# Attention and two gated MLPs on one core: scores in three 64-row passes, sums unfolded, another clock in the planner

## The chip, the cores and the metric

The kernel runs on one core of one Trainium2 chip. The metric is the time of one execution on the device, in microseconds (us). The engines are TensorE (PE in the profile, PEld for its weight loads), VectorE (DVE), ScalarE (ACT), GpSimd (POOL) and SyncE (SP), whose queue issues nearly all DMAs.

## What is computed

The inputs are q, k and v for 4 batches, 12 heads, 448 positions and a head size of 64, in float32. The reference, cut to what matters:

```python
q_n, k_n = rmsnorm(q, g_q), rmsnorm(k, g_k)          # x / sqrt(mean(x*x)+1e-6) * g
attn = softmax(q_n @ k_n.T / 8)
x = (attn @ v), heads side by side                    # 4 x 448 x 768
h = relu(x @ w_in); c = conv over 3 positions of h    # d_ff 1024
x = (h * sigmoid(c)) @ w_out
g = sigmoid(causal conv over 5 positions of x)
out = (g * (x @ w_val)) @ w_out2
```

## The kernel before

Products are taken in float16 with each operand split in a high and a low part: high times high, high times low and low times high are summed in PSUM.

Heads are handled in pairs. A *unit* is 128 query rows of a pair of heads (kind "full", 72 units) or the last 64 rows of two pairs (kind "rem", 12 units); there are 21 units in each of the 4 batches. `prep` makes q and k ready for two pairs: it loads them, sums their squares (`sum_q`, `sum_k`), takes the inverse root in a few steps on VectorE (`rroot`), multiplies k with the gains and its root (`gain_k`, `norm_k`), and splits q and k in halves (`split_q`, `norm_k`, `low_k`). DMA transposes (`turn_q`, `turn_k`) bring them to the layout with the head dimension on partitions: `qa` and `ka`. In `norm_k` the high part of k is copied a second time, so that each head's column block of `ka` has it on rows 0 to 63 and again on rows 64 to 127; `qa` has for each head q's high and low part under each other, so one matmul over 128 rows gives high k times (high q + low q). `qk` issues this for both heads, and then the low part of k times high q over 64 rows, for one head on rows 0 to 63 and for the other on rows 64 to 127. It writes to one of two PSUM buffers, `ps_s`, with one bank for each head.

`sum_q` and `sum_k` square on ScalarE or GpSimd and call `total`. With FOLD_Q = FOLD_K = 2 `total` first adds halves of the 64 squares on GpSimd, twice, and reduces the 16 that are left on VectorE. The first group of pairs, marked solo, isn't folded.

After the scores, `smax` takes the negative maximum on VectorE, `sexp` the exponential on ScalarE. For a unit with `u.out` set, the exponentials go to an SBUF buffer, `phi` copies them to float16 and `plo` subtracts on VectorE or GpSimd; otherwise the exponentials overwrite the scores in PSUM, and `plo` is a VectorE instruction that reads PSUM. OUT = (0, 4, 4, 4) sets `u.out` for all units of batches 1 to 3. The units of batch 0 are `wide`: their probabilities stay in float32 and TensorE transposes them. In the other batches DMA transposes turn p into `pt`, and `av` multiplies with v. The MLP of batch b runs beside the attention of batch b+1; the MLP of batch 3 runs alone.

The order of the instructions is made by the program itself, on the host, in the class `Plan`. Every instruction is recorded with the time at which the program wants it. `order` is a list scheduler: it keeps a clock for each engine with an estimated duration for each instruction (`cost`), and lets each engine take the ready instruction with the smallest value of `first`, a mix of the wanted time and of the length of the chain behind it (URGENT). Instructions given for two engines go to the one that would end sooner, with a lean. A change of matmul shape on TensorE is made less likely by SWITCH. `clocked` models the granted clock. The result is one fixed queue for each engine, in which every instruction waits for those ahead of it. All these instructions have line 351 in the profile, since `emit` issues them there.

Of the kernel before, what the change touches and what calls it, by code (L numbers as in the profile page):

```python
# [9 lines left out]
F32 = mybir.dt.float32  # L10
F16 = mybir.dt.float16
# [14 lines left out]
class Plan:  # L26
# [10 lines left out]
    HOP = {"tensor": 0.2, "vector": 0.13, "scalar": 0.16, "gpsimd": 0.09}  # L37
    WINDOW = 23.2
    AHEAD = 55.6
    URGENT = 0.598  # L40
    TICK = 10.24 / 3
    ENTRY = 3060.0

    SWITCH = 3.692

    KEEP = 0.1
# [123 lines left out]
    def cost(self, engine, method, a, k, aps, out):  # L170
# [63 lines left out]
    def order(self):  # L234
        ops, nops = self.ops, len(self.ops)
        users = [[] for _ in ops]
        left = [len(o[1]) for o in ops]
        for i, o in enumerate(ops):
            for d in o[1]:
                users[d].append(i)  # L240
        ready = [o[2] for o in ops]
        tail = [0.0] * nops
# [12 lines left out]
        first = [o[4] * (1.0 - self.URGENT) - tail[i] * self.URGENT for i, o in enumerate(ops)]  # L255
        waiting = {e: [] for e in Plan.ENGINES}
        free = dict.fromkeys(Plan.ENGINES, 1.05)
# [22 lines left out]
        while len(result) < nops:  # L280
# [36 lines left out]
            if method.startswith("dma"):  # L317
                if e != "gpsimd":
                    t = max(since + 0.03 if e == "scalar" else t, ready[i], hwdge)
                    hwdge = t + lag + 0.03  # L320
                    busy = max(free[e] - t, lag + 0.05)
                    dma = max(dma, hwdge + 0.62)
                    if method == "dma_start_transpose":
                        busy = max(1.22, dma + 0.69 - t if data > 1.0 else 0.0)
                    dma += data
                else:
                    dma = max(dma, t + 3.4) + data
                end = dma + (0.7 if k["out"].space == bass.MemoryType.DRAM else 1.5)
            else:
                end = t + busy + lag  # L330
            if e == "scalar":
                since = t
            free[e] = t + busy
            if port[i][e]:
                held[e] = t + busy - (0.06 if e == "vector" else 0.09)
            result.append((t, len(result), i, e))
            for u in users[i]:
# [3 lines left out]
                if left[u] == 0:  # L341
                    enter(u)
        self.length = max(free.values())
        self.times = {i: t for t, _, i, _ in result}
        self.engine = {i: e for _, _, i, e in result}
        return [(i, e) for _, _, i, e in result]

# [7 lines left out]
def kernel(  # L355
# [43 lines left out]
    wo, wv, w2 = (sb.tile([P, 2 * n, DM], F16, tag=t, name=t) for t, n in (("wo", KF), ("wv", KD), ("w2", KD)))  # L399
    ka = tiles(NKA, [P, 3, S], F16, "ka")  # L400
    qa = tiles(2, [P, NQ, P], F16, "qa")
    vvf = tiles(NV, [P, 2 * NB * (D + 1)], F16, "vv")
# [9 lines left out]
    qin = tiles(1, [P, NQ, D], F32, "qin")  # L412
    tk = tiles(1, [KR, 3, KC, 2 * D], F16, "tk")
    tq_ = tiles(1, [P, NQ, 2 * D], F16, "tq")
    p32 = tiles(2, [P, 2, S], F32, "p32_")
# [55 lines left out]
    START = 8.8  # L471
    HOLD = 12.4
    EARLY_W = 19
# [17 lines left out]
    C_LO = 3.1  # L491
    V_HI = 0.971
    A_HI = 0.836
    A_LO = 1.248
    A_OUT = 0.192
    E_PTR = 0.83
    E_AV = 2.135
    X_LAG = 1.732
    MPE = 96.0
    M_0 = 2.65  # L500
    M_1 = 0.311
    M_2 = 0.038
    M_3 = -1.7
    D_IN = 3.4
    L_TAP = 0.0
    L_DUP = 4.061
# [8 lines left out]
    D_OUT = 4.34  # L515
    D_VAL = 3.58
    D_Y = 2.44
    KLEAD = 3.645
    QLEAD = 3.741
    VLEAD = 5.37  # L520
    STAT = 0.341
    KD_ = 1.21
    QD_ = 1.09
    W_IN = -69.458
    W_IN_STEP = 1.774
    W_OUT = -16.897
    W_OUT_STEP = 2.33
    W_VAL = 30.678
    W_VAL_STEP = 2.16
    W_2 = 85.7  # L530
    W_2_STEP = 3.998
# [5 lines left out]
    BIG_2 = 0  # L537
    OUT = (0, 4, 4, 4)
    WIDE_0 = 1
# [7 lines left out]
    L_WLO = 0.899  # L547
    L_ROOT = 0.3
    L_QHI = 0.729
    L_QLO = 0.968  # L550
    L_GAIN = 1.72
    L_NORM = 4.34
    L_KHI = 1.361
    L_KLO = 0.76
    L_PLO = 0.5
    L_VM = 0.001
    L_VHI = 1.224
    L_VLO = 1.058
    L_PHI = 1.118
    L_PT = 4.0  # L560
    L_XHI = -0.2
    L_GHI = 1.0

# [58 lines left out]
    for i in range(EARLY):  # L622
        free.remove(i)
    tk.append(slot(0, 3)[:KR, 0 : 12 * 2 * D].rearrange("p (a c d) -> p a c d", a=3, c=KC))
    early_sq = slot(3, 2).bitcast(F32)
# [155 lines left out]
    def prep(b, r, t0, tq, dq, tk_, dk, ahead):  # L781
# [16 lines left out]
        n = 4 * FULL  # L798
        oh = oq.rearrange("p (n h) (a d) -> p n (h a) d", h=2, a=2)[:, :, 0:4:3]
        gain_b = gb[0][:KR].unsqueeze(1).to_broadcast([KR, 2 * KC, D])  # L800
# [25 lines left out]
        def sum_q():  # L826
            s2 = early_sq if b == 0 else oq.rearrange("p n d -> p (n d)").bitcast(F32)
            s2 = s2.rearrange("p (n d) -> p n d", d=D)
            square(s2, xq)
            total(FOLD_Q, ss[:, 0:NQ], s2)  # L830

        def split_q():
            x = xq.rearrange("p (n h) d -> p n h d", h=2)
            copy(lean(L_QHI, S_LQ), oh, x)
            sub(lean(L_QLO, S_LQ), oq.rearrange("p (n x) d -> p n (x d)", x=2)[:, :, D : 3 * D].rearrange("p n (h d) -> p n h d", h=2), x, oh)

        def turn_q():
            nc.sync.dma_start_transpose(out=qa[g % 2], in_=oq.rearrange("p n d -> p (n d)"))

        def of_k(i):  # L840
            j = 2 * r + i
            x = kin[i]
            o = tk[i if b == 0 else 0]
            return j, x, x.rearrange("p h c d -> p (h c) d"), o, o[:, 0:2]

# [5 lines left out]
        def sum_k(i):  # L851
            j, x, x3, o, hi = of_k(i)
# [11 lines left out]
        def norm_k(i):  # L864
            j, x, x3, o, hi = of_k(i)
            assert holds["kin", i] == (b, j)
            holds["tk", i if b == 0 else 0] = b, j
            vg(lean(L_NORM, S_LK), "tensor_tensor", x3, x3, rr[:KR, cols(i)].unsqueeze(2).to_broadcast([KR, 2 * KC, D]), ALU.mult)
            copy(lean(L_KHI, S_LK), hi[:, :, :, 0:D], x)
            copy(lean(L_DUP, S_LK), hi[:, :, :, D : 2 * D], hi[:, :, :, 0:D])  # L870

        def low_k(i):
            j, x, x3, o, hi = of_k(i)
            assert holds["kin", i] == holds["tk", i if b == 0 else 0] == (b, j)
            sub(lean(L_KLO, S_LK), o[:, 2].rearrange("p c (h d) -> p h c d", h=2), x, hi[:, :, :, 0:D])

        def turn_k(i):
            j, x, x3, o, hi = of_k(i)
# [628 lines left out]
```

## Time and profile before

| | |
|---|---|
| three timed runs | 697.35 us median, 695.71 to 697.99 |
| the profiled execution | 692.04 us, of which 689.8 us is the span of the core |
| granted TensorE clock, mean | 0.955 of full speed |
| TensorE | 589.4 us busy (85% of the span), 4562 matmuls |
| VectorE | 508.4 us (74%), 1072 instructions |
| ScalarE | 432.9 us (63%), 751 |
| GpSimd | 300.7 us (44%), 328 |

A busy time counts the instructions that an engine executes, and for VectorE this includes time in which an instruction has begun and waits inside. The records of successive matmuls overlap, so the price of one is read from the start of one to the start of the next and not from its duration.

### The profile page before, as it was taken

What the parts mean: (1) busy time and instruction counts of PE and PEld (TensorE: products, weight loads), DVE (VectorE), ACT (ScalarE), POOL (GpSimd) and SP (SyncE); (2) the same over time, 40 slices, a digit from 0 to 9 for tenths busy, and PEclk for the clock granted to TensorE, in tenths of its full rate; (3) what the DMA queues carried; (4) which work ended last, traced back from release to release, by engine and by line L of the source; (5) the groups of instructions that cost most, each with busy time, mean ns of one, the idle gap of its engine ahead of it and who ended that gap; (6) DMA issues with size and microseconds to landing.
All of it is one profiled execution on the core that took longest, in us unless ns stands there. A gap on an engine that the chain in (4) does not pass through costs nothing. (4 is left out here: it accounts for less than half of the span.)

```text
span 689.8 us, 12402 instructions
## 1 busy us (share of the span) xinstructions
PE 589.4 (85%) x4562; PEld 333.8 (48%) x4562; DVE 508.4 (74%) x1072; ACT 432.9 (63%) x751; POOL 300.7 (44%) x328
## 2 busy tenths in 40 slices
PE   0579888957787898786989899999999899999997
PEld 0447766434343344343545454654554456545554
DVE  5888977998998877889728586459889763586720
ACT  3588988886886964786837575577856543342211
POOL 3376366666476675564756644441653110000000
PEclk9997999989898999979999999999999999999999
DMA  8968576968977985985978758865836736100001
GB/s 203 219 158 202 126 183 141 219 127 158 219 158 160 234 151 120 193 183 120 168 168 176 123 106 139 164 126 112 146 67 113 115 54 153 35 1 0 1 21 60
DMA packets 269324, 91.76 MB, mean 133 GB/s; under 512 B 255387, under 2 KB 265169, under 8 KB 269265
## 3 DMA queue, kind: packets, MB, share of 16 engines
q1 hardware_dynamic: 268353, 90.76, 63.6%
q8 instruction: 35, 0.57, 0.3%
q10 hardware_dynamic: 912, 0.23, 0.1%
q14 instruction: 24, 0.20, 0.1%
HBM read 38.66 MB, written 5.51 MB: 64 GB/s over the span
## 5 line engine op out<-in xcount | busy, mean ns | idle before, releaser
L351 PE MATMUL psm<-act,wi 128*128 128x448 f16 x576 | 124.2, 363 | 8.9 <-DVE act L351 8.8
L351 ACT ACTIVATE p<-pss,mx,root 128x448 f32<-128x448 f32 x154 | 103.5, 721 | 38.7 <-POOL mx L351 18.7
L351 PE MATMUL psm<-act,wo 128*128 128x448 f16 x576 | 121.7, 358 | 1.6 <-DVE act L351 1.6
L351 PE MATMUL pss<-ka,qa 128*128 128x448 f16 (+3 forms) x384 | 84.4, 376 | 32.2 <-DMA ka<-tk 20.0
L351 DVE TENSOR_REDUCE pss<-pss 128x2 f32<-128x896 f32 x84 | 90.9, 1091 | 24.0 <-PE pss L351 21.5
L351 POOL TENSOR_TENSOR p<-p,p 128x896 f16<-128x896 f32 x41 | 77.7, 1895 | 50.1 <-ACT p L351 38.5
L351 PE MATMUL psm<-act,wv 128*128 128x448 f16 x432 | 92.9, 362 | 5.9 <-DVE act L351 5.9
L351 PE MATMUL psm<-w,act 128*128 128x384 f16 (+1 forms) x576 | 93.2, 327 | 0.9 <-DVE act L351 0.9
L351 ACT ACTIVATE act<-psm 128x448 f16<-128x448 f32 (+4 forms) x97 | 51.4, 536 | 61.2 <-DVE psm L351 42.3
L351 PEld LDWEIGHTS <-wi 128*128 128x128 f16 x576 | 55.9, 100 | 61.9 <-issue 18.2
L351 PEld LDWEIGHTS <-pt 128*128 128x128 f16 (+1 forms) x1512 | 59.5, 103 | 50.4 <-DMA pt<-p 32.0
L351 PEld LDWEIGHTS <-wo 128*128 128x128 f16 x576 | 55.1, 99 | 54.6 <-issue 9.3
L351 PE MATMUL psx<-vv,pt 128*128 128x65 f16 (+1 forms) x1116 | 71.5, 207 | 0.4 <-ACT pt L351 0.4
L351 PEld LDWEIGHTS <-act 128*128 128x128 f16 (+1 forms) x576 | 48.7, 101 | 33.2 <-issue 4.3
L351 DVE SCALAR_TENSOR_TENSOR act<-psm,cw,act 128x444 f32<-128x444 f32 (+3 forms) x96 | 63.7, 676 | 1.0
L351 PEld LDWEIGHTS <-wv 128*128 128x128 f16 x432 | 41.9, 100 | 45.1 <-issue 12.0
L351 PEld LDWEIGHTS <-qa 128*128 128x128 f16 (+3 forms) x384 | 25.3, 100 | 76.1 <-issue 47.6
L351 ACT ACTIVATE p<-p 128x896 f16<-128x896 f32 x62 | 58.9, 950 | 1.8 <-DMA pt<-p 1.3
L351 DVE SCALAR_TENSOR_TENSOR w<-w 128x768 uint32<-128x768 uint32 (+1 forms) x56 | 47.9, 866 | 0.6 <-POOL w L351 0.4
L351 DVE SCALAR_TENSOR_TENSOR scr<-psm,cw,scr 128x447 f32<-128x447 f32 x64 | 43.0, 677 | 4.4 <-ACT scr L351 3.7
L351 PE MATMUL psx<-vm,pt 128*128 128x130 f16 (+1 forms) x186 | 25.1, 241 | 22.2 <-DMA pt<-p 15.7
L351 DVE SCALAR_TENSOR_TENSOR act<-psm,act 128x448 f16<-128x448 f32 x48 | 29.7, 618 | 12.6 <-ACT act L351 12.5
(122 smaller groups left out, 906.0 us busy)
## 6 DMA issues: line engine op xcount, KB each, us to landing
w<-in_moe_w_in_dram SPq DMA_DIRECT2D x8, 768.0 KB, 6.4
w<-in_moe_w_out_dram SPq DMA_DIRECT2D x8, 768.0 KB, 5.9
kin<-in_k_dram SPq DMA_DIRECT2D x23, 224.0 KB, 3.6
qin<-in_q_dram SPq DMA_DIRECT2D x36, 128.0 KB, 3.2
act<-in_moe_w_out_dram SPq DMA_DIRECT2D x12, 384.0 KB, 3.4
w<-in_moe_w_val_dram SPq DMA_DIRECT2D x12, 384.0 KB, 3.9
out_dram<-osb SPq DMA_DIRECT2D x24, 192.0 KB, 2.5
vst<-in_v_dram SPq DMA_DIRECT2D x18, 224.0 KB, 4.3
```

The costliest lines, as they stand in the source:

```text
L351: getattr(getattr(nc, e), method)(*a, **k)
```

## The change

`qk` issues three steps of two matmuls: (high q, high k), (low q, high k), (high q, low k), each over 64 rows for the first head and 64 rows for the second. `ka` has two blocks instead of three, the copy of k's high part is gone, and q's halves lie in two plain blocks. FOLD_Q and FOLD_K are 0, OUT is (0, 0, 4, 4). In the planner, the costs of DMAs are other numbers with issue and landing apart, GpSimd's own DMA branch is gone, and `order` runs the list scheduler PASSES = 4 times: after each it computes backwards from the result the latest start of each instruction and mixes this into `first` with the weight 1 - MIX = 0.2; the shortest result is kept. Some 35 constants of wanted times and leans change by small amounts. Cut to its core:

```diff
-    WINDOW = 23.2
+    WINDOW = 23.016
-    URGENT = 0.598
+    URGENT = 0.584
+    PASSES = 4
+    MIX = 0.8
...
         if method.startswith("dma"):
-            data = k["in_"].nbytes() / 292e3
             if method == "dma_start":
-                data = k["in_"].nbytes() / (360e3 if k["in_"].shape[-1] * 4 >= 512 else 180e3)
-                return 1.1 if engine == "gpsimd" else 0.5, 0.46, data
-            return 1.2, 0.63, data
+                data = k["in_"].nbytes() / (330e3 if k["in_"].shape[-1] * 4 >= 512 else 180e3)
+                return 0.5, 2.15 + data - 0.2 * (out.space == bass.MemoryType.DRAM), data
+            data = k["in_"].nbytes() / 230e3
+            return 1.1 + 0.22 * data, 2.3 + 0.92 * data, data
...
-            if self.region(out)[0]:
+            if self.region(out)[0] or (a[1].shape[0] == 64 and self.region(a[2])[0]):
                 return 0.022, f * n * a[1].shape[0] / 256, 0
...
+        best = None
+        for _ in range(self.PASSES):
+            result, length, ends = self.forward(first, users, port, shape)
+            if best is None or length < best[1]:
+                best = result, length
+            late = self.backward(result, length, ends, users)
+            first = [self.MIX * a + (1.0 - self.MIX) * b for a, b in zip(first, late)]
...
+    def backward(self, result, length, ends, users):
+        late = [length] * len(self.ops)
+        free = dict.fromkeys(self.ENGINES, length)
+        for t, _, i, e in reversed(result):
+            end, busy = ends[i]
+            last = min((late[u] for u in users[i]), default=length) - (end - t)
+            late[i] = min(last, free[e] - busy)
+            free[e] = late[i]
+        return late
...
-    FOLD_Q = 2
-    FOLD_K = 2
+    FOLD_Q = 0
+    FOLD_K = 0
...
-    OUT = (0, 4, 4, 4)
+    OUT = (0, 0, 4, 4)
...
-            copy(lean(L_KHI, S_LK), hi[:, :, :, 0:D], x)
-            copy(lean(L_DUP, S_LK), hi[:, :, :, D : 2 * D], hi[:, :, :, 0:D])
+            copy(lean(L_KHI, S_LK), hi, x)
...
-        for low in range(2):
+        steps = ((0, 0), (1, 0), (0, 1))
+        for n, (a, w) in enumerate(steps):
             for hh in range(2):
-                rows = slice(hh * D, (hh + 1) * D) if low else slice(0, P)
+                rows = slice(hh * D, (hh + 1) * D)
                 for (p0, m, j, idx) in parts:
                     nc.tensor.matmul(
                         ps[p0 : p0 + m, hh, 0:S],
-                        qa[(u.b * NPR // 2 + u.r) % 2][rows, idx(hh), p0 : p0 + m],
-                        ka[(u.b * NPR + j) % NKA][rows, 2 if low else hh],
-                        start=not low,
-                        stop=bool(low),
+                        qa[(u.b * NPR // 2 + u.r) % 2][rows, a, idx(0) // 2, p0 : p0 + m],
+                        ka[(u.b * NPR + j) % NKA][rows, w],
+                        start=n == 0,
+                        stop=n == len(steps) - 1,
                     )
```

## Rows read from the trace of the kernel before

**Rows 1.** Windows: stretch, length, each engine's busy us (count), clock, DMA share, GB/s.
```profile
20.00:121.00 101.00, 82.09 (x604) 62.87 (x603) 84.40 (x190) 82.82 (x146) 58.65 (x67) 0.92 0.73 170
121.00:268.00 147.00, 117.31 (x928) 58.89 (x927) 129.32 (x262) 112.29 (x196) 95.08 (x93) 0.90 0.83 175
268.00:345.00 77.00, 62.84 (x486) 34.01 (x484) 65.14 (x141) 56.20 (x104) 45.47 (x45) 0.91 0.80 160
345.00:447.00 102.00, 94.59 (x820) 52.52 (x818) 61.58 (x145) 59.63 (x100) 53.00 (x55) 1.00 0.78 146
447.00:586.00 139.00, 132.54 (x1165) 72.58 (x1164) 101.35 (x202) 85.71 (x145) 42.81 (x44) 1.00 0.60 111
```

**Rows 2.** Waits of TensorE, 120 to 345 us: total us, times, longest.
```profile
PE psm L351 <- DVE act L351: 16.9, 11, 3.3
PE pss L351 <- ACT p L351: 9.6, 7, 4.8
```

**Rows 3.** Waits of all engines, whole span.
```profile
PE psx L351 <- DMA pt<-p: 15.7, 17, 4.3
```

**Rows 4.** Timeline of TensorE, 400 to 412 us: start, duration, what.
```profile
401.60 0.36 PE L351 MATMUL pss<-ka,qa 64*128 64x448 f16 x2
401.89 0.35 PE L351 MATMUL psx<-vm,pt 128*128 128x130 f16 x3
...
403.95 0.35 PE L351 MATMUL pss<-ka,qa 128*128 128x448 f16 x1
404.14 3.38 PE L351 MATMUL psm<-act,wv 128*128 128x448 f16 x17
```

**Rows 5.** Timeline of TensorE, 86.0 to 87.2 us.
```profile
86.35 0.55 PE L351 MATMUL pss<-ka,qa 64*128 64x448 f16 x4
86.83 0.44 PE L351 MATMUL psm<-vm,act 128*64 128x130 f32 x4
```

**Rows 6.** Groups by form, VectorE: count, busy us, mean ns, idle before; sums of squares.
```profile
L351 DVE TENSOR_REDUCE ssq<-tk 112x8 f32<-112x128 f32 x18 | 5.0, 280 | 14.9 <-POOL tk L351 14.9
...
L351 DVE TENSOR_REDUCE ssq<-tq 128x14 f32<-128x224 f32 x9 | 3.4, 377 | 1.1 <-POOL tq L351 1.1
...
L351 DVE TENSOR_REDUCE ssq<-act 112x8 f32<-112x512 f32 x2 | 1.4, 678 | 0.0
...
L351 DVE TENSOR_REDUCE ssq<-act 128x14 f32<-128x896 f32 x1 | 1.1, 1086 | 0.8 <-ACT act L351 0.8
```

**Rows 7.** Groups by form, GpSimd: the first folds.
```profile
L351 POOL TENSOR_TENSOR tk<-tk 112x256 f32<-112x256 f32 x18 | 14.1, 781 | 23.1 <-ACT tk L351 23.0
...
L351 POOL TENSOR_TENSOR tq<-tq 128x448 f32<-128x448 f32 x9 | 11.1, 1235 | 6.4 <-ACT tq L351 6.3
```

**Rows 8.** Groups by form, ScalarE: the second copy of k's high part.
```profile
L351 ACT ACTIVATE tk<-tk 112x512 f16<-112x512 f16 x20 | 12.6, 630 | 0.2
```

**Rows 9.** Timeline of all engines, 0 to 26 us.
```profile
13.63 0.29 DVE L351 COPY tk<-tk 112x512 f16<-112x512 f16 x1
...
18.47 2.51 PE L351 MATMUL pss<-ka,qa 128*128 128x448 f16 x8 [18.47 <-DMA ka<-tk]
```

**Rows 10.** DMA issues: count, median us from issue to landing.
```profile
act<-x SPq DMA_TRANSPOSE x36, 2.6
ka<-tk SPq DMA_TRANSPOSE x21, 3.7
```

**Rows 11.** Groups by form, VectorE, 120 to 262 us.
```profile
L351 DVE TENSOR_TENSOR p<-p,p 128x896 f16<-128x896 f32 x5 | 5.4, 1082 | 0.0
L351 DVE SCALAR_TENSOR_TENSOR half<-root 128x30 f32<-128x30 f32 x7 | 4.3, 608 | 0.0
```

**Rows 12.** Groups by form, GpSimd, 120 to 262 us.
```profile
L351 POOL TENSOR_TENSOR p<-p,p 128x896 f16<-128x896 f32 x15 | 28.6, 1909 | 8.2 <-ACT p L351 8.2
```

**Rows 13.** The tile half on VectorE: ns min/median/max, first and last start.
```profile
L351 DVE SCALAR_TENSOR_TENSOR half<-root x42: 160/182/1874, 8.3 to 508.7; 128x30 f32<-128x30 f32 x33, 112x8 f32<-112x8 f32 x6, 128x14 f32<-128x14 f32 x3
```

**Rows 14.** Groups by form, VectorE: a subtraction that reads PSUM.
```profile
L351 DVE SCALAR_TENSOR_TENSOR act<-psm,act 128x448 f16<-128x448 f32 x48 | 29.7, 618 | 12.6 <-ACT act L351 12.5
```

More of the change, by code (lines that the diff above doesn't have):

```diff
@@ L236, in order @@
         users = [[] for _ in ops]
-        left = [len(o[1]) for o in ops]
         for i, o in enumerate(ops):
@@ L240, in order @@
                 users[d].append(i)
-        ready = [o[2] for o in ops]
         tail = [0.0] * nops
@@ L255, in order, with forward @@
         first = [o[4] * (1.0 - self.URGENT) - tail[i] * self.URGENT for i, o in enumerate(ops)]
+        best = None
[5 more added lines that the diff above has]
+            first = [self.MIX * a + (1.0 - self.MIX) * b for a, b in zip(first, late)]
+        result, self.length = best
+        self.times = {i: t for t, _, i, _ in result}
+        self.engine = {i: e for _, _, i, e in result}
+        return [(i, e) for _, _, i, e in result]
+    def backward(self, result, length, ends, users):
[7 more added lines that the diff above has]
+        return late
+    def forward(self, first, users, port, shape):
+        ops, nops = self.ops, len(self.ops)
+        left = [len(o[1]) for o in ops]
+        ready = [o[2] for o in ops]
+        ends = [None] * nops
         waiting = {e: [] for e in Plan.ENGINES}
@@ L317, in order @@
             if method.startswith("dma"):
[L318 to L328, printed above, removed]
+                t = max(since + 0.03 if e == "scalar" else t, ready[i], hwdge)
+                hwdge = t + 0.45
+                behind = max(dma - t - 1.28, 0.0)
+                dma = t + 1.28 + behind + data
+                end = t + lag + (0.8 if method == "dma_start_transpose" else 1.0) * behind
+                busy += (0.35 if method == "dma_start_transpose" else 0.08) * behind
+                busy = max(free[e] - t, busy)
             else:
@@ L333, in order @@
             free[e] = t + busy
+            ends[i] = end + (0.0 if method.startswith("dma") else self.HOP[e]), busy
             if port[i][e]:
@@ L342, in order @@
                     enter(u)
[L343 to L346, printed above, removed]
+        return result, max(free.values()), ends
     def emit(self, nc):
@@ L399 @@
     wo, wv, w2 = (sb.tile([P, 2 * n, DM], F16, tag=t, name=t) for t, n in (("wo", KF), ("wv", KD), ("w2", KD)))
-    ka = tiles(NKA, [P, 3, S], F16, "ka")
-    qa = tiles(2, [P, NQ, P], F16, "qa")
+    ka = tiles(NKA, [P, 2, S], F16, "ka")
+    qa = tiles(2, [P, 2, NQ // 2, P], F16, "qa")
     vvf = tiles(NV, [P, 2 * NB * (D + 1)], F16, "vv")
@@ L412 @@
     qin = tiles(1, [P, NQ, D], F32, "qin")
-    tk = tiles(1, [KR, 3, KC, 2 * D], F16, "tk")
-    tq_ = tiles(1, [P, NQ, 2 * D], F16, "tq")
+    tk = tiles(1, [KR, 2, KC, 2 * D], F16, "tk")
+    tq_ = tiles(1, [P, 2, NQ * D], F16, "tq")
     p32 = tiles(2, [P, 2, S], F32, "p32_")
@@ L471 @@
     START = 8.8
-    HOLD = 12.4
+    HOLD = 12.186
     EARLY_W = 19
@@ L491 @@
     C_LO = 3.1
-    V_HI = 0.971
-    A_HI = 0.836
+    V_HI = 0.934
+    A_HI = 0.853
     A_LO = 1.248
@@ L497 @@
     E_AV = 2.135
-    X_LAG = 1.732
+    X_LAG = 1.873
     MPE = 96.0
-    M_0 = 2.65
+    M_0 = 2.641
     M_1 = 0.311
-    M_2 = 0.038
-    M_3 = -1.7
+    M_2 = 0.001
+    M_3 = -1.725
     D_IN = 3.4
-    L_TAP = 0.0
-    L_DUP = 4.061
+    L_TAP = -0.036
     LATE = 1
     LATE_F = 12
-    FOLD_Q = 2
-    FOLD_K = 2
+    FOLD_Q = 0
+    FOLD_K = 0
     SIGN_IN = 1
@@ L514 @@
     SIGN_2 = 0
-    D_OUT = 4.34
+    D_OUT = 4.105
     D_VAL = 3.58
     D_Y = 2.44
-    KLEAD = 3.645
+    KLEAD = 3.457
     QLEAD = 3.741
@@ L522 @@
     KD_ = 1.21
-    QD_ = 1.09
-    W_IN = -69.458
+    QD_ = 1.359
+    W_IN = -70.745
     W_IN_STEP = 1.774
-    W_OUT = -16.897
+    W_OUT = -14.821
     W_OUT_STEP = 2.33
@@ L529 @@
     W_VAL_STEP = 2.16
-    W_2 = 85.7
+    W_2 = 87.193
     W_2_STEP = 3.998
@@ L547 @@
     L_WLO = 0.899
-    L_ROOT = 0.3
+    L_ROOT = 0.317
     L_QHI = 0.729
-    L_QLO = 0.968
-    L_GAIN = 1.72
+    L_QLO = 0.933
+    L_GAIN = 1.803
     L_NORM = 4.34
-    L_KHI = 1.361
+    L_KHI = 1.296
     L_KLO = 0.76
@@ L556 @@
     L_VM = 0.001
-    L_VHI = 1.224
-    L_VLO = 1.058
+    L_VHI = 0.976
+    L_VLO = 1.051
     L_PHI = 1.118
-    L_PT = 4.0
+    L_PT = 4.056
     L_XHI = -0.2
-    L_GHI = 1.0
+    L_GHI = 0.496
     WIDE = [(0, r) for r, w in enumerate((WIDE_0, WIDE_1, WIDE_2)) if w]
@@ L623 @@
         free.remove(i)
-    tk.append(slot(0, 3)[:KR, 0 : 12 * 2 * D].rearrange("p (a c d) -> p a c d", a=3, c=KC))
+    tk.append(slot(0, 3)[:KR, 0 : 8 * 2 * D].rearrange("p (a c d) -> p a c d", a=2, c=KC))
     early_sq = slot(3, 2).bitcast(F32)
@@ L798, in prep @@
         n = 4 * FULL
-        oh = oq.rearrange("p (n h) (a d) -> p n (h a) d", h=2, a=2)[:, :, 0:4:3]
         gain_b = gb[0][:KR].unsqueeze(1).to_broadcast([KR, 2 * KC, D])
@@ L826, in sum_q @@
         def sum_q():
-            s2 = early_sq if b == 0 else oq.rearrange("p n d -> p (n d)").bitcast(F32)
+            s2 = early_sq if b == 0 else oq.rearrange("p a n -> p (a n)").bitcast(F32)
             s2 = s2.rearrange("p (n d) -> p n d", d=D)
@@ L832, in split_q @@
         def split_q():
-            x = xq.rearrange("p (n h) d -> p n h d", h=2)
-            copy(lean(L_QHI, S_LQ), oh, x)
-            sub(lean(L_QLO, S_LQ), oq.rearrange("p (n x) d -> p n (x d)", x=2)[:, :, D : 3 * D].rearrange("p n (h d) -> p n h d", h=2), x, oh)
+            x = xq.rearrange("p n d -> p (n d)")
+            copy(lean(L_QHI, S_LQ), oq[:, 0], x)
+            sub(lean(L_QLO, S_LQ), oq[:, 1], x, oq[:, 0])
         def turn_q():
-            nc.sync.dma_start_transpose(out=qa[g % 2], in_=oq.rearrange("p n d -> p (n d)"))
+            nc.sync.dma_start_transpose(out=qa[g % 2].rearrange("p a n t -> p (a n) t"), in_=oq.rearrange("p a n -> p (a n)"))
         def of_k(i):
@@ L843, in of_k @@
             o = tk[i if b == 0 else 0]
-            return j, x, x.rearrange("p h c d -> p (h c) d"), o, o[:, 0:2]
+            hi, lo = [o[:, a].rearrange("p c (h d) -> p h c d", h=2) for a in range(2)]
+            return j, x, x.rearrange("p h c d -> p (h c) d"), o, hi, lo
         def load_k(i):
@@ L851, in sum_k @@
         def sum_k(i):
-            j, x, x3, o, hi = of_k(i)
+            j, x, x3, o, hi, lo = of_k(i)
             assert holds["kin", i] == (b, j)
@@ L864, in norm_k @@
         def norm_k(i):
-            j, x, x3, o, hi = of_k(i)
+            j, x, x3, o, hi, lo = of_k(i)
             assert holds["kin", i] == (b, j)
```

6 lines of the change are left out of this document (3 added, 3 removed).

## The prediction

> **What bounds the kernel now.** I read the time by stage first. The stages were found from where each weight's matmuls begin: attention of batch 0 alone until 121 us, then the first MLP beside attention 1 until 268, the second MLP's first product until 345, then the rest, and from 586 us the last MLP alone. The reader is to see two regimes in [rows 1]. From 345 us on, TensorE is busy 93 to 95% of the time at a granted clock of 1.00; VectorE has 60 to 73%, so there only TensorE's own work counts. Before 345 us TensorE is busy for about 80% and its clock is 0.90 to 0.92, so some of its work runs at 1.2 GHz; VectorE is the fullest engine, at 129.32 of 147 us (88%) in the stage from 121 us. What can be won lies there: 1 minus the granted clock, times the stage, is 8.1 + 14.7 + 6.9 = 29.7 us, and TensorE stands idle for 18.9 + 29.7 + 14.2 = 62.8 us.
>
> Second, who keeps TensorE waiting. From 120 to 345 us the largest single cause is VectorE's low halves of the MLP activations (16.9 us), then ScalarE's exponentials that still hold a score buffer (9.6 us) [rows 2]. Over the whole run the transposed probabilities come late 17 times, 15.7 us in all [rows 3].
>
> The sum is made against the profiled execution, 692.04 us, of which 689.8 is span. The three timed runs have their median at 697.35 us; I add this difference of 5.3 us at the end.
>
> **Scores.** A full unit now has two matmuls on 128 rows (k's high part stands twice, q's high and low part under each other) and one pair on 64 rows, one head in each half of the array. After, it has three such pairs. The timeline shows the price of each: a 128-row matmul of 448 columns at 403.95 is followed after 0.19 us (404.14); a 64-row pair at 401.60 is followed by a 128-row matmul after 0.29 us (401.89) [rows 4]. So the pair's two matmuls run at once, and leaving the mode costs 0.10; I put entering at 0.10 too. Two pairs behind each other, four matmuls, start at 86.35 and the next group starts at 86.83: 0.48, that is 0.19 for the first pair and 0.29 for the last [rows 5]. Before: 2 x 0.19 + 0.29 + 0.10 = 0.77 us. After, with the pairs in one block: 0.10 + 2 x 0.19 + 0.29 = 0.77 us. I take 0. The low bound is -2 us, since the 12 units of remaining rows use one tile shape instead of two. The high bound is three lone pairs in each unit, two extra mode changes of 0.20 each: 84 x 0.4 = +34 us. I take the block, because the list order adds a penalty for a change of shape (SWITCH) in both directions, which keeps the six together once all are ready.
>
> The Trainium skill, TensorEngine Tiling (Array Packing), section Key Properties, says that changing the tiling mode drains TensorE. The trace agrees, with the 0.10 us above; by that rule alone this change is as good as its blocks are whole, and the sum would be 0 or the +34 us just given.
>
> **k without its double.** The copy that doubles k's high part goes: 20 ScalarE activations of 0.630 us, 12.6 us, and a few elsewhere [rows 8]. The k transpose shrinks from 1536 to 1024 columns. It lands after 3.7 us, one of 384 columns after 2.6 [rows 10]; on that line 512 columns are worth 1.1 x 512/1152 = 0.49 us, an estimate. At the start both stand before the first score at 18.47 us, with the copy there at 0.29 us [rows 9]: 0.8 us; I take -0.7, bounds -0.8 and 0, as the q transpose is ahead in the same queue. Later k is made ahead and hidden under the units of the pair before; if that cover is gone, the 1.1 us of copy and landing come off each late k.
>
> **Sums unfolded.** GpSimd loses its folds: 14.1 us for the first fold of k and 11.1 us for that of q [rows 7], the second folds on top. VectorE pays in its reductions: 0.678 for 0.280 us for each k, 1.086 for 0.377 us for each q [rows 6]. With 22 folded k and 11 folded q that is 22 x 0.40 + 11 x 0.71 = 16.6 us more on VectorE over the run, about 11 of it before 345 us. After 345 us VectorE has the room. Against this stands that VectorE waits for GpSimd inside its own instructions: the steps of the root on 30 columns take 0.182 us in the median and up to 1.874 [rows 13], which is the length of a GpSimd subtraction (1.909) [rows 12]; seven of them in the stage average 0.608, a loss of 7 x 0.43 = 3.0 us [rows 11]. Together with the ScalarE time won I take -4 us for folds and copy; bounds -12 (the waits of TensorE for VectorE fall by two thirds) and +6 (half of the 11 us shows).
>
> The Trainium skill, GPSIMD Engine Reference, section Specifications, has GpSimd's SBUF interfaces shared with VectorE, contended by VectorE instructions with two SBUF inputs or in a two-port mode. The two-input root steps that reach 1.874 us agree with it. By it the reductions, with one input, cost their plain 16.6 us and every fold that goes returns some time.
>
> **Batch 1's probabilities stay in PSUM.** OUT goes from 4 to 0 for batch 1, so its 21 units write exp into the score bank, and the low half is a VectorE operation only. In the stage GpSimd did 15 of them at 1.909 us [rows 12] and VectorE 5 [rows 11]. VectorE gets 15 x 1.082 = 16.2 us more (2 x 0.618 each, the row of the same form at half the width, would make 18.5 [rows 14]). GpSimd, at 95 of 147 us, loses 28.6. It also adds a wait: the scores of unit n+2 now wait until VectorE has read the bank for unit n, 1.08 us for the subtraction [rows 11] and a copy in front of it later than the exponentials release it, some 2 us, an estimate. Behind such a score in TensorE's queue stand the MLP's products, and VectorE's convolutions wait for these. The stage has 147/21 = 7.0 us a unit and two banks, so 14 us a bank against a use of some 6; that slack hides it. Bounds -4 and +17 (worked out as a rival); I take +2, as VectorE is nearly full but its subtraction is 0.8 us quicker than GpSimd's.
>
> **The order.** The planner is run four times, with each operation's urgency mixed with its latest start from the pass before, and the shortest plan is kept; DMA costs are issue and landing. SP is one queue in order, so a better clock for its transfers moves transposes past loads. Nothing of this can be priced from a row. What it can win is bounded by the 15.7 us of late transposes [rows 3], the 26.5 us of [rows 2] and the 29.7 us of low clock [rows 1], 72 us; I take a tenth or so, -8 us, bounds -20 and +8, since a list order may as well put a transpose behind a blocked one.
>
> **Sum.** 0 - 0.7 - 4 + 2 - 8 = -10.7, so 681.3 us for a profiled execution, and 681.3 + 5.3 = 686.6, call it 687 us. The likeliest case's own range is 680 to 694.
>
> **Rivals.** (1) VectorE becomes the bound of 121 to 268 us, and the kernel is slower. Busy there 129.3; add 16.2, and 3 q and 6 k reductions of this stage (4.5); take off 6 for waits on GpSimd that vanish (twice the 3.0 shown, an estimate): 144 of 147 us. If VectorE can fill no more than its 88%, the stage grows by 14.7/0.88 = 16.7 us. With the other terms at -12.7 that is 697.35 + 4 = 701; with the order's gain at zero, 709. It decides once VectorE must be over about 95% busy. For it: the low halves of VectorE are already what TensorE waits for most. Against: GpSimd and ScalarE have room for whatever either can do.
> (2) No change: order and relief move idle time about, and TensorE's work after 345 us is the same; 697.
> (3) The order wins more: the stages before 345 us lose half of their low-clock time (15 us) and 7 us of the late transposes; 697.35 - 22 = 675. For it: the low clock comes with TensorE idle, so one gives the other. Against: VectorE's sum.
> (4) The scores' pairs don't stay together: a third of the 34 us, some 11, half of it behind TensorE's full stages, undoes the gain; 692. It is inside my range.
>
> **Chances.** Forecast, with (4) in it, 0.49; (3) 0.13; (2) 0.13; (1) 0.25. Faster by over 0.3% (2.1 us, about what can be told from no change) 0.62, within 0.13, slower 0.25. Range 674 to 703: it holds the forecast, (2), nearly all of (3), and about half of (1).
>
> **What will show it.** Right: scores as blocks of six 64-row matmuls with 0.19 us between pairs; no GpSimd folds; the first score near 17.8 us; the stage from 121 us no longer than 147 with VectorE above 90%; fewer waits for transposed probabilities; granted clock above 0.92 before 345 us. Wrong: that stage longer and score matmuls waiting for VectorE's reads of the bank, or scores scattered as lone pairs after 345 us.

## The result, and the profile after

The kernel after takes 672.42 us (median of 4 runs, 672.01 to 673.07), the kernel before 697.67 us in the same job: a ratio of 0.9644, with a 95% interval of 0.9624 to 0.9665. The forecast was 687 us with a range of 674 to 703: the direction was right, the time lies 1.6 us below the range, and the gain of 25.3 us is over twice the 10.7 us of the sum. The profiled executions are 692.04 us before and 672.69 us after, 19.4 us apart. The traces can explain only these 19.4; in the rest, before's profiled execution was 5.6 us quicker than its timed runs. Single executions of before went from 688.2 to 701.6 us in the later jobs, so both its numbers are ordinary ones; the kernel after was not timed in another job.

**Where the time went.** Four stages of the MLP, with the matmuls that start first and last: the first product of the first MLP, the first and the third of the second, the first of the last. The columns are the shortest, median and longest duration in ns, the start of the first and of the last of them, and the form. Before, and then after:

```profile
L351 PE MATMUL psm<-act,wi x144: 349/353/581, 121.0 to 178.8; 128*128 128x448 f16 x144
...
L351 PE MATMUL psm<-act,wi x144: 349/352/581, 267.9 to 329.9; 128*128 128x448 f16 x144
...
L351 PE MATMUL psm<-act,wv x108: 350/352/353, 399.8 to 424.6; 128*128 128x448 f16 x108
...
L351 PE MATMUL psm<-act,wi x144: 349/352/362, 588.2 to 616.5; 128*128 128x448 f16 x144
```
```profile
L374 PE MATMUL psm<-act,wi x144: 349/352/581, 114.8 to 168.3; 128*128 128x448 f16 x144
...
L374 PE MATMUL psm<-act,wi x144: 350/352/581, 264.7 to 321.5; 128*128 128x448 f16 x144
...
L374 PE MATMUL psm<-act,wv x108: 350/352/363, 384.4 to 411.8; 128*128 128x448 f16 x108
...
L374 PE MATMUL psm<-act,wi x144: 349/352/362, 569.0 to 597.3; 128*128 128x448 f16 x144
```

The lead is 6.2 us when the first MLP begins, 3.2 us when the second begins, 12.8 us at the end of the second MLP's third product, and 19.2 us when the last MLP begins; that MLP takes 101.6 us before and 101.5 after. The steps between these marks depend on which products an order puts first, so they don't date the gain exactly; but part of it comes after 345 us, where I had put next to nothing. In all, TensorE's idle time falls from 100.4 to 90.2 us and its busy time by 9.1.

The windows of [rows 1], after, in the same columns and at the same times (the work itself stands up to 19 us further on):

```profile
20.00:121.00 101.00, 80.85 (x683) 60.25 (x678) 89.97 (x197) 85.11 (x149) 43.72 (x50) 0.95 0.77 175
121.00:268.00 147.00, 122.46 (x1031) 62.37 (x1031) 135.64 (x279) 112.37 (x201) 58.55 (x53) 0.88 0.89 176
268.00:345.00 77.00, 61.67 (x511) 33.30 (x511) 62.22 (x136) 57.94 (x104) 41.66 (x39) 0.93 0.83 172
345.00:447.00 102.00, 99.48 (x900) 55.44 (x899) 72.43 (x152) 56.73 (x95) 33.84 (x33) 1.00 0.69 137
447.00:586.00 139.00, 134.44 (x1176) 73.31 (x1175) 101.47 (x201) 73.56 (x126) 36.36 (x34) 1.00 0.50 92
```

From 121 us VectorE now works 135.64 of 147 us, 92%, and TensorE is busy 5 us longer there, part of it because its clock is 0.88 there instead of 0.90: the engine that I feared as the bound took the load. GpSimd falls from 95.08 to 58.55 us. From 345 to 447 us TensorE's share rises from 93 to 98%. TensorE's idle time from 345 to 586 us falls from 13.9 to 7.1 us, and from 20 to 345 us only from 62.8 to 60.0. The clock's share hardly moves (0.95, 0.88 and 0.93 before 345 us, where it was 0.92, 0.90 and 0.91).

TensorE's waits over the whole run, before and then after; [rows 2] showed those of 120 to 345 us, [rows 3] the wait for `pt`:

```profile
PE psm L351 <- DVE act L351: 19.7, 19, 3.3
...
PE pss L351 <- ACT p L351: 10.0, 8, 4.8
PE psm L351 <- ACT p L351: 9.9, 5, 6.2
```
```profile
PE psx L374 <- DMA pt<-p: 24.3, 20, 5.4
...
PE psm L374 <- DVE act L374: 10.7, 11, 2.9
PE pss L374 <- ACT p L374: 6.0, 2, 4.9
...
PE psm L374 <- ACT p L374: 5.2, 3, 3.9
PE pss L374 <- DVE p L374: 2.6, 1, 2.6
```

The waits for transposed probabilities did not fall, they rose from 15.7 to 24.3 us. Those for VectorE's low halves fell from 19.7 us to 10.7, and those for ScalarE's exponentials from 19.9 to 11.2. The wait that OUT adds, scores behind VectorE's reading of the bank, is there once, for 2.6 us.

The scores, timelines of TensorE after:

```profile
357.76 0.92 PE L374 MATMUL psm<-act,wo 128*128 128x448 f16 x4
358.61 1.31 PE L374 MATMUL pss<-ka,qa 64*128 64x448 f16 x12
359.85 0.36 PE L374 MATMUL psm<-vm,pt 128*64 128x130 f16 x6
...
387.07 0.74 PE L374 MATMUL pss<-ka,qa 64*128 64x448 f16 x6
387.74 0.74 PE L374 MATMUL psm<-act,wv 128*128 128x448 f16 x3
```

One unit's block of three pairs takes 0.67 us to the next matmul, 2 x 0.19 + 0.29 as worked out from [rows 4, 5], and entering costs the 0.10 that was put for it (four matmuls of 0.19 take 0.85 us from 357.76 to 358.61). So a single block costs 0.77 us, as forecast. But two units share a block in 1.24 us, which saves one entering and leaving, 0.20 us. Over the whole run TensorE's matmuls change from one tile form (rows by columns) to another 223 times before and 170 times after: 53 x 0.10, some 5 us less, an estimate. The forecast of 0 left this out.

The sums and the transposes, after: groups by form, DMA issues, and the timeline of the start.

```profile
L374 DVE TENSOR_REDUCE ssq<-tk 112x8 f32<-112x512 f32 x18 | 12.2, 679 | 2.9 <-ACT tk L374 2.8
...
L374 DVE TENSOR_REDUCE ssq<-tq 128x14 f32<-128x896 f32 x9 | 9.7, 1075 | 0.0
```
```profile
ka<-tk SPq DMA_TRANSPOSE x21, 3.2
```
```profile
14.62 0.52 SPq L374 DMA_DIRECT2D qin<-in_q_dram  x1
15.25 1.22 SPq L374 DMA_TRANSPOSE ka<-tk  x1
...
18.36 2.05 PE L374 MATMUL pss<-ka,qa 64*128 64x448 f16 x10 [18.36 <-DMA ka<-tk]
```

The reductions cost what [rows 6] said, and the 14.9 us that VectorE stood idle for folds of k are gone. The k transpose lands after 3.2 us, as estimated from [rows 10]. Yet the first score comes only 0.1 us sooner than in [rows 9]: the transpose was issued at 15.25 us, behind a load of q, where before it was issued at 14.86. The step came out near 0, the high one of its bounds.

### The profile page after: what moved, and what is told of

Its sections match the earlier page's. It is cut to its first block, busy times and chain, and to the rows that moved or that the text cites. A ratio compares the mean times of both kernels' runs of the same rounds, so it can differ in the third digit from the quotient of the medians.

```text
span 670.5 us, 12665 instructions
## 1 busy us (share of the span) xinstructions
PE 580.3 (87%) x4754; PEld 328.2 (49%) x4754; DVE 518.4 (77%) x1079; ACT 415.2 (62%) x726; POOL 220.5 (33%) x235
## 4 chain that ended last, share of the span: by engine, by line
PE 48%; DVE 18%; DMA 14%; ACT 8%; issue 5%; POOL 4%; SPq 2%; POOLq 0%; ACTq 0%; DVEq 0%
PE psm L374 38%; DMA pt<-p 11%; PE psx L374 6%; PE pss L374 4%; DVE act L374 4%; DVE scr L374 3%; DVE pss L374 3%; ACT p L374 3%; SPq L374 2%; DVE w L374 2%; ACT act L374 2%; POOL p L374 2%; DVE p L374 1%; DMA w<-in_moe_w_out_dram 1%; DVE psm L374 1%
## 5 line engine op out<-in xcount | busy, mean ns | idle before, releaser
L374 PEld LDWEIGHTS <-pt 128*128 128x128 f16 (+1 forms) x1512 | 68.7, 102 | 63.3 <-DMA pt<-p 42.0
L374 PE MATMUL pss<-ka,qa 64*128 64x448 f16 (+1 forms) x576 | 69.3, 376 | 34.3 <-DMA ka<-tk 18.6
L374 ACT ACTIVATE p<-pss,mx,root 128x448 f32<-128x448 f32 x112 | 75.1, 725 | 32.7 <-DVE mx L374 21.9
L374 PE MATMUL psx<-vv,pt 128*128 128x65 f16 (+1 forms) x1116 | 87.3, 206 | 0.0
L374 POOL TENSOR_TENSOR p<-p,p 128x896 f16<-128x896 f32 x26 | 49.7, 1910 | 60.1 <-ACT p L374 43.8
L374 DVE SCALAR_TENSOR_TENSOR act<-psm,cw,act 128x446 f32<-128x446 f32 (+3 forms) x96 | 64.0, 676 | 1.0
L374 PEld LDWEIGHTS <-wv 128*128 128x128 f16 x432 | 41.7, 100 | 44.7 <-issue 12.8
L374 PEld LDWEIGHTS <-qa 64*128 64x128 f16 (+1 forms) x576 | 23.1, 100 | 67.6 <-issue 27.1
L374 PE MATMUL psx<-vm,pt 128*128 128x130 f16 (+1 forms) x186 | 27.3, 242 | 25.1 <-DMA pt<-p 24.3
L374 DVE SCALAR_TENSOR_TENSOR w<-w 128x768 uint32<-128x768 uint32 (+1 forms) x56 | 44.1, 789 | 0.1
L374 POOL TENSOR_TENSOR kin<-kin,gb 112x512 f32<-112x512 f32 x22 | 30.2, 1376 | 37.0 <-ACT act L374 18.6
L374 ACT ACTIVATE osb<-psm 128x384 f32<-128x384 f32 x28 | 13.6, 490 | 42.7 <-PE psm L374 41.0
```

The lines of the kernel that those rows point to most:

```text
L374: getattr(getattr(nc, e), method)(*a, **k)
```

## The experiments

Each time is the median beside that of before on the same chip; since that one varies from job to job, each on its own chip (692.9 to 695.8 us, and 697.67 in the job of after), the ratios to before are what compares, with their 95% intervals. In ratios, after stands at 0.9644. Its own interval holds for its one job only; so where a run is set against after, the difference of the times, which leaves before out, is given too. Three theories run through them: A, the planner's new clock and passes made the order better; W, the work taken away made the room; F, any order is good only with constants that were fitted to it. In the expectations of e1 to e4 W is called B, F is called D, and C is A and B together; W1 and W2 are W with most of the gain in the sums or in the scores.

**Planner and data path, each alone.** e1: after with planner class, constants, FOLD and OUT of before.

```diff
-    PASSES = 4
-    MIX = 0.8
...
-    W_OUT = -14.821
+    W_OUT = -16.897
...
-    FOLD_Q = 0
+    FOLD_Q = 2
-    OUT = (0, 0, 4, 4)
+    OUT = (0, 4, 4, 4)
```

> Edit: the kernel after with the planner, the constants, FOLD and OUT of before; what is left of the change is the data path alone: three 64-row passes, k's high part not doubled, plain halves of q (the planner knows that a 64-row pair runs at once). Theory A (the order): these parts are worth no more than the 0.7 us of the start, so 694 to 700 us. Theory B (the work taken away): copy, shorter transposes and blocks of scores are a third of the 25 us, so 687 to 691 us.

706.17 us beside 694.38, ratio 1.0175 (1.0134 to 1.0217): a miss for both. e2: before with the planner class of after.

```diff
+    PASSES = 4
+    MIX = 0.8
...
+            data = k["in_"].nbytes() / 230e3
+            return 1.1 + 0.22 * data, 2.3 + 0.92 * data, data
...
```

> Edit: the kernel before with the planner class of after (DMA costs, four passes, WINDOW, URGENT), everything else as before. Theory A (the order): it brings most of the 25 us, so 675 to 682 us. Theory B (the work taken away): the order alone brings little, 692 to 699 us. Theory C (it takes both, as the order could only win where engines have room): 685 to 691 us, and more from the two together than the sum of the two alone.

709.46 us, ratio 1.0218 (1.019 to 1.0245), again slower, outside all three. e3: after with the planner class of before, which is told that a 64-row pair runs at once.

```diff
-    PASSES = 4
-    WINDOW = 23.016
+    WINDOW = 23.2
...
```

> Edit: the kernel after with the planner class of before (one pass, DMA costs, WINDOW and URGENT of before), knowing of the row pairs. Theory A (the order): the gain is lost, 690 to 698 us. Theory B (the work taken away): 674 to 680 us. Theory C (both): 680 to 690 us.

690.06 us, 0.9942 (0.9911 to 0.9973), on the border of A and C. e4: after, with the 24 wanted times and leans in which the kernels differ beside FOLD and OUT (I had said some 35) set as before.

```diff
-    W_IN = -70.745
+    W_IN = -69.458
-    L_GHI = 0.496
+    L_GHI = 1.0
...
```

> Edit: the kernel after with the 24 wanted times and leans of before (WINDOW and URGENT among them), FOLD, OUT and planner as after. Theory A (the order): the planner's clock does the work and the constants are small change, 672 to 679 us. Theory D (the constants are fitted to one order, and any other order is several us worse): 680 to 690 us.

691.61 us, 0.995 (0.9915 to 0.9985), a little above D's range: of after's gain 3 points in 3.6 are gone with nothing changed but small shifts of constants. Half-changed kernels are all worse than after, and two of them worse than before. So these four runs don't divide the gain; they suggest that an order and its constants belong together. Two kinds of run that do divide it followed: the order held fixed while work is put in or left out, and each variant with its constants searched anew for the shortest plan on the planner's own clock (a random search on the host, before the run).

**The order held fixed.** e5: before's order, folds left out when issued, reductions over 64. e6: after's order, folds put back in front of the reductions. The first lines of the diff are e5's, the others e6's.

```diff
+            if i in self.gone:
+                continue
...
+                    for d in (32, 16):
+                        real.gpsimd.tensor_tensor(x[:, :, 0:d], x[:, :, 0:d], x[:, :, d : 2 * d], ALU.add)
...
+                nc.swap[len(nc.ops) - 1] = (out, x[:, :, 0:16], AX.X, ALU.add)
```

> Edit: the kernel before with its order of instructions kept as it is; only when the instructions are issued, the 66 folds on GpSimd are left out and each reduction on VectorE takes all 64 squares. Same result. Theory W (the work taken away is worth something by itself): the folds stood in the chain from the load of k and q to the scores and on the port that VectorE shares, so 685 to 692 us. Theory F (the gain is in how well the constants fit the order): a fixed order can't use it and VectorE pays 16.6 us, 694 to 700 us.

> Edit: the kernel after with its order kept; when the instructions are issued, the two folds on GpSimd are put in front of each reduction (not for the first group), which then takes 16 sums. Same result. Theory W: GpSimd gets about 45 us back, 680 to 690 us. Theory F: GpSimd has room (33% busy), 672 to 676 us.

e5: 695.76 us beside 693.02, 1.003 (0.9991 to 1.0068), no change, as F said. e6: 702.65 us, 1.0132 (1.0063 to 1.0201), 5% over after (4.5% by the times), far above both expectations. Groups by form of e6, VectorE:

```profile
L379 DVE TENSOR_REDUCE ssq<-tk 112x8 f32<-112x128 f32 x18 | 5.1, 285 | 35.0 <-POOL tk L842 35.0
...
L379 DVE TENSOR_REDUCE ssq<-tq 128x14 f32<-128x224 f32 x9 | 3.4, 382 | 7.9 <-POOL tq L842 7.9
```

VectorE now stands 42.9 us in front of reductions whose folds aren't done, and everything in its queue stands behind. This is more than folds need cost: here they are issued right in front of their reduction, while in before, where the planner placed them, the same two rows have 16.0 us [rows 6]. e15 takes this wait away and keeps the load: at the same places of GpSimd's queue it makes the same additions on a spare buffer.

```diff
+                    y = spare[:m, 0 : n * D].rearrange("p (n d) -> p n d", d=D)
+                    for d in (32, 16):
+                        real.gpsimd.tensor_tensor(y[:, :, 0:d], y[:, :, 0:d], y[:, :, d : 2 * d], ALU.add)
```

> Edit: the kernel after with its order kept; at the places in GpSimd's queue where the folds stood in the run with folds put back, GpSimd does the same additions on a spare buffer that nobody waits for, and the reductions take all 64 squares. Same result. If the folds cost by GpSimd's load and by the port that it shares with VectorE, 690 to 700 us, as with the folds put back. If they cost because VectorE stands behind them in order, 674 to 680 us.

686.11 us beside 693.16, 0.9893 (0.9846 to 0.9939), 2.6% over after (2.0% by the times): half of what e6 lost, between the two expectations. Busy times of the page, after, e15, e6 and e5:

```profile
PE 580.3 (87%) x4754; PEld 328.2 (49%) x4754; DVE 518.4 (77%) x1079; ACT 415.2 (62%) x726; POOL 220.5 (33%) x235
```
```profile
PE 586.4 (86%) x4754; PEld 332.9 (49%) x4754; DVE 544.1 (79%) x1079; ACT 415.6 (61%) x726; POOL 272.3 (40%) x302
```
```profile
PE 597.8 (85%) x4754; PEld 342.2 (49%) x4754; DVE 516.3 (73%) x1079; ACT 416.8 (59%) x726; POOL 265.6 (38%) x301
```
```profile
PE 594.2 (85%) x4562; PEld 336.4 (48%) x4562; DVE 518.4 (74%) x1072; ACT 432.8 (62%) x751; POOL 250.9 (36%) x262
```

In e15 VectorE executes the same 1079 instructions as after and is busy 25.7 us longer, for 51.8 us more of GpSimd. That is not a fixed toll. With the folds themselves (e6) GpSimd works 45.1 us longer than after, and VectorE's instructions other than the reductions, which are 16.3 us shorter there, grow by some 14 us. In e5 GpSimd works 49.8 us less than in before, and the same part of VectorE's time falls by 6.4 us only (10.0 us more in all, 16.4 of them reductions).

The instructions that stretch in e15 read two operands from SBUF, or are `TENSOR_SCALAR`, `COPY` and `CAST` from SBUF to SBUF; the reductions and all that touch PSUM keep their time. Of the weights' bit operations, the root's steps and the reduction of the scores, after and e15:

```profile
L374 DVE SCALAR_TENSOR_TENSOR w<-w 128x384 uint32<-128x384 uint32 x24 | 13.8, 573 | 0.0
...
L374 DVE SCALAR_TENSOR_TENSOR half<-root 128x30 f32<-128x30 f32 x33 | 8.3, 250 | 0.4
...
L374 DVE TENSOR_SCALAR half<-ssq 128x30 uint32<-128x30 uint32 x11 | 2.5, 230 | 1.2 <-POOL ssq L374 1.2
...
L374 DVE TENSOR_REDUCE pss<-pss 128x2 f32<-128x896 f32 x84 | 90.8, 1092 | 23.4 <-PE pss L374 23.3
```
```profile
L379 DVE SCALAR_TENSOR_TENSOR w<-w 128x384 uint32<-128x384 uint32 x24 | 15.9, 660 | 0.0
...
L379 DVE SCALAR_TENSOR_TENSOR half<-root 128x30 f32<-128x30 f32 x33 | 11.2, 338 | 0.4
...
L379 DVE TENSOR_SCALAR half<-ssq 128x30 uint32<-128x30 uint32 x11 | 5.8, 523 | 5.9 <-POOL ssq L379 5.9
...
L379 DVE TENSOR_REDUCE pss<-pss 128x2 f32<-128x896 f32 x84 | 90.8, 1091 | 21.3 <-PE pss L379 21.3
```

What e15 loses in time is not all by this stretching: the rest of GpSimd's queue stands behind the additions too, as the 5.9 us show that VectorE waits for GpSimd's `ssq`. The run doesn't part the two.

e7: after's order with the second copy of k's high part back on ScalarE, into a spare buffer.

```diff
+            nc.behind[len(nc.ops) - 1] = [lambda real: real.scalar.activation(spare, o[:, 0]..., AF.Copy)]
```

> Edit: the kernel after with its order kept; behind each of the 24 copies of k's high part ScalarE makes one more copy of it, into a spare buffer that nobody reads. Same result. Theory W: 24 x 0.63 = 15 us of ScalarE, 62% busy, show by a quarter to a half, 676 to 680 us. Theory F: hidden, 672 to 674 us.

676.49 us, 0.9754 (0.9704 to 0.9804), 1.1% over after, but only 4.1 us (0.6%) by the times: 24 copies, 14 us of ScalarE (415.2 to 429.3 us busy), show by a quarter to a half, as W said.

**Each variant with a search of its own.** The diffs are the switches named and a handful of constants, as in e12, which is after with seven constants searched on:

```diff
-    WINDOW = 23.016
+    WINDOW = 22.9735
-    W_OUT = -14.821
+    W_OUT = -9.8103
-    L_GHI = 0.496
+    L_GHI = 1.2638
...
```

> Edit: the kernel after with FOLD_Q and FOLD_K back at 2, and its 24 wanted times and leans searched anew for the shortest plan by the planner's own clock, so that this variant has an order fitted to it too. Theory W: the folds cost what no order hides, 681 to 688 us. Theory F: any data path can be fitted, 671 to 677 us.

> Edit: the kernel after with OUT back at (0, 4, 4, 4) for batch 1, and the 24 constants searched anew for the shortest plan, as for the variant with folds. If the move of batch 1's low halves to VectorE is worth its 2 us either way, 670 to 675 us. If it is a cause of the gain, 678 to 685 us.

> Edit: the kernel before (its data path, folds and OUT) with the planner class of after, and the constants searched anew for the shortest plan. Theory W (the data path is worth most, once both have a fitted order): 688 to 698 us. Theory A (the planner's new clock is what counts): 674 to 682 us.

> Edit: the kernel after with the planner class of before (one pass, old DMA costs; it knows of the row pairs), and the constants searched anew for the shortest plan by that clock. Theory W: with the data path of after and a fitted order, 670 to 677 us. Theory A (the new clock is needed to find a good order): 683 to 690 us, as with the old planner and constants not searched.

> Edit: the kernel after, its 24 constants searched on for the shortest plan by its own clock. If the planner's clock is true to the chip to about 3 us, 668 to 672 us and the fastest of all. If its last microseconds are only fitted to the clock and not to the chip, 671 to 678 us.

> Edit: the kernel after with FOLD 2 and OUT (0, 4, 4, 4) as before, so that of the data path only the score passes and the single copy of k are new; planner of after, constants searched anew for the shortest plan. The old data path with the same planner and a search had a ratio of 1.005 to before, that of after 0.954. Theory W1 (the unfolded sums are most of it): 0.985 to 1.0, 684 to 695 us. Theory W2 (the scores and the copy are most of it): 0.96 to 0.975, 667 to 678 us.

> Edit: the kernel before with FOLD 0, the planner of after and constants searched anew for the shortest plan; scores, copy of k and OUT as before. Theory W1 (unfolded sums): 0.965 to 0.98, 670 to 681 us. Theory W2 (scores and copy): 0.99 to 1.005, 687 to 699 us.

> Edit: the kernel after with PASSES = 1, constants searched anew for the shortest plan. If the four passes bring something that no search brings, 672 to 680 us; if not, as after with searched constants, 660 to 670 us.

> Edit: as the unfolded sums alone (data path of before with FOLD 0, planner of after), with a second, independent search of the constants. If unfolding alone is worth nothing on the chip, again 0.995 to 1.005 of before, 689 to 700 us. If the first order was unlucky, 0.97 to 0.99, 675 to 688 us.

> Edit: the kernel after with constants searched anew, started from those of before and with other random numbers; this order has nothing of the one of after. If the data path of after carries the gain whatever the order, once searched, 0.95 to 0.975 of before, 660 to 680 us. If the order of after is a lucky one, 0.975 to 0.99, 680 to 690 us.

| run | scores in passes, one copy of k | sums unfolded | batch 1 in PSUM | planner | us | ratio, 95% |
|---|---|---|---|---|---|---|
| e10 | no | no | no | after | 699.30 | 1.005 (1.0014 to 1.0087) |
| e13 | yes | no | no | after | 694.96 | 1.003 (0.9994 to 1.0066) |
| e14 | no | yes | no | after | 692.35 | 0.9996 (0.9966 to 1.0027) |
| e17 | no | yes | no | after | 689.40 | 0.9942 (0.9901 to 0.9982) |
| e8 | yes | no | yes | after | 687.92 | 0.9931 (0.99 to 0.9962) |
| e9 | yes | yes | no | after | 677.48 | 0.975 (0.9703 to 0.9797) |
| e12 | yes | yes | yes | after | 662.62 | 0.9536 (0.9478 to 0.9594) |
| e18 | yes | yes | yes | after | 676.22 | 0.9728 (0.9665 to 0.979) |
| e16 | yes | yes | yes | after, one pass | 674.37 | 0.9723 (0.9661 to 0.9785) |
| e11 | yes | yes | yes | before | 669.01 | 0.9627 (0.9563 to 0.969) |

Against the expectations: e8 and e18 came out as W said, e10 a little above W's range and e11 a little below it (e11's four runs go from 664 to 680 us, so its place is loose). e9 lies between its two, e12 below both. e16 fell where the four passes were to bring something; but e18, with four passes, has the same ratio, so the runs don't show that. e13 came out as if the sums were most of the gain and e14 as if the scores were, and e17 repeats e14 to half a point: neither alone brings the gain.

Theory A falls: the planner of after on the old data path brings nothing (e10), and the planner of before on the new one keeps the gain (e11), as does a single pass (e16). W stands: all orders with the whole new data path lie between 0.954 and 0.973, five with after's own among them, a mean of 0.965. By their diffs the searches on the old scores began from before's constants and the others from after's, all but e18, which began from before's and keeps the gain. The scatter of two points is what is left of F: one search's order is worth a per cent more or less than another's on the chip, the differences between chips included. Taking one part away from that mean costs, for the folds (e8) 2.8 points, for the passes and the single copy together with batch 1 (e14, e17) 3.2, for batch 1 alone (e9) 1.0, which is inside the scatter. Yet, counted from e10, the passes with folds kept (e13) gain 0.2 points and unfolded sums alone 0.8 in the mean, while both together (e9) gain 3.0. Every searched order with both stands at 0.975 or below, every one that lacks one of them at 0.993 or above. So the two seem to need each other; but the excess of 2.0 points is no more than the scatter of orders, and these runs don't settle it. No searched order parts the passes from the single copy of k.

e12 is faster than both kernels. It did not run beside after; through before, it stands at 0.9536/0.9644 = 0.989 of it.

## Why the prediction was wrong

**Sums unfolded and the single copy, -4 us: mis-sized, and the main error.** This term stood for folds and copy together, with -12 as its bound, and the scores had 0. From e10 to e9, which differ in just these edits and in searched constants, the gain is 3.0 points, 21.8 us between their medians in one job. How it divides is open. On the old scores unfolding brings 0.8 points, some 6 us, about what I had put; on the new ones the folds cost 2.8 points, some 19 us (e8). I added prices that were taken one by one from the kernel before, and neither the sum nor the bound of -12 left room for edits that are worth more together, which is how these runs look, though they don't prove it.

Of what folds cost, two things show in the traces. VectorE's queue stands still in front of a reduction while GpSimd folds; [rows 6] show this in the column that I did not use, 14.9 and 1.1 us, and e8 has it again:

```profile
DVE ssq L374 <- POOL tk L374: 10.9, 5, 4.8
```

GpSimd's own queue stood 23.1 and 6.4 us in front of the folds, waiting for ScalarE [rows 7]; what that cost no run shows. The other thing is the port, for which I estimated 6 us of relief in the stage. From before to after VectorE's busy time rose by 10.0 us, where the reductions (16.6) and batch 1's subtractions (16.2) should have made 32.8, so 22.8 us came back, though other instructions changed engines as well. But e5, with nothing else changed, gives back 6.4 us, and e15 takes 25.7 for the same load in another order. So the port's share of the folds' 19 us is not shown.

The Trainium skill's rule, weighed there from GPSIMD Engine Reference, section Specifications, that GpSimd's SBUF interfaces are shared with VectorE, agrees with e15: 25.7 us of VectorE for 51.8 of GpSimd, and two-input instructions among those that stretched.

**The order, -8 us: the other wrong step.** The clock with measured DMA times and the four passes bring nothing that the runs can show (e10, e11, e16). I bounded the order's gain by waits for transposed probabilities, and these rose. An order whose constants don't fit it loses 3 points, some 20 us (e4); that a good order turns room on the engines into time is my reading, and no run shows it by itself.

**Batch 1 in PSUM, +2 us.** Its sign was perhaps wrong: -1.0 points (e9), about 7 us, though within the scatter of orders. The rival that made VectorE the bound was to decide at 95%; VectorE reached 92%.

**Scores, 0 on TensorE.** Right to 0.01 us for a single block, and rival (4), scattered pairs, hardly happened (about ten of the 84 units are split in two). But the fewer changes of tile form were left out, some 5 us. The busy time agrees: of the 9.1 us that TensorE has less, 1 minus the mean granted clock (0.955 and 0.959), times the span, makes 3.5 us, and 5.6 are left for its work, an estimate. And the copy of k that goes with them was priced as hidden beyond the start: its ScalarE time shows by 4 to 7 us when it is put back (e7), as much as the whole joint -4.

**The stages.** That after 345 us only TensorE's own work counts was too simple: its idle time from 345 to 586 us fell by 6.8 us, more than before 345, and I had left it out of the sum. Of the signs that I listed, the blocks, the missing folds and VectorE above 90% came true; the fewer waits for transposes, the clock above 0.92, the stage from 121 us (149.9 us by the marks above, 146.9 before) and the first score at 17.8 us did not. Rival (3) had 675 us, the number nearest to the result, but by luck: the clock and the late transposes that were to give it did not change that way.

**The 5.3 us.** I carried before's distance between profiled and timed execution over to after. It was no property of the program: before's own timed medians were 692.9 to 695.8 us in the later jobs, so its profiled execution was an ordinary one, and after's profiled execution, one of its timed runs, is 0.3 us from their median. Without it the sum says 681.3 us, 8.9 off.

## What to carry to other kernels

Price an instruction on GpSimd by what stands behind it: the engine that waits in order for its result, and the VectorE instructions that share its port, not by GpSimd's own free time. When several edits make room on different engines, don't take the sum of their single prices for the price of all: leave a bound for their working together. In a kernel whose order is made by a planner, judge a change only with the order made anew and its constants searched for that variant; half a change with the other half's constants misleads by 3%. And read the idle column of a row whose busy time you quote.

## What the runs showed of the hardware

GpSimd's elementwise additions on 112 to 128 partitions lengthened VectorE's instructions, by 25.7 us for 51.8 us of additions where nobody waited for them (e15), by some 14 for 45.1 where VectorE did (e6); leaving 49.8 us of them out of another order gave back 6.4 (e5). In e15 the growth lies in VectorE instructions that read two operands from SBUF (14 us) and in `TENSOR_SCALAR`, `COPY` and `CAST` from SBUF to SBUF (13 us, in sums by form); reductions (120 us) and instructions that touch PSUM took the same time to 0.1 us.

Successive 64-row pairs of matmuls, 448 columns each, keep 0.19 us from pair to pair up to six pairs in a row, with all weight loads hidden; entering and leaving such a block costs 0.10 us each.
